# Windowed attention with sinks and an MLP on one core: scores and values of batches 2 to 4 in one run of 64x64 quarters

## The chip, the core and the metric

The kernel runs on one core of a Trainium2 chip. The metric is the device time of one execution in microseconds. TensorE (PE) multiplies matrices; VectorE (DVE), ScalarE (ACT) and GpSimd (POOL) work on elements; SyncE (SP) and POOL issue most of the DMA transfers. Below, a *quarter* is a matmul whose weights are 64 rows by 64 columns; TensorE's array of 128 by 128 holds four of them side by side (two row halves, two column halves).

## The reference

```python
batch, n_heads, seq, head_dim = (4, 8, 768, 64)
n_sink, window = (4, 128)
...
scores = scale * np.matmul(q, k.transpose(0, 1, 3, 2))
keep = is_sink | in_window        # key < 4, or 0 <= query - key < 128
scores = np.where(keep, scores, -1000000000.0)
a = softmax(scores)
attn = np.matmul(a, v)            # heads side by side: x is [4, 768, 512]
...
xn = (x - mu) / np.sqrt(var + 1e-06) * g_ln
ch = np.maximum(xn @ w_ch1, 0.0) @ w_ch2     # 512 -> 2048 -> 512
return (x + ch).astype(np.float32)
```

Each query sees its own and at most the 127 keys before it, and the four sink keys at the start of the sequence.

## The kernel before

A *tile* is 128 positions of one batch with all 8 heads (24 tiles, six to a batch); a *chunk* c is two tiles (12 chunks, three to a batch, R = c % 3). Batch 1 is chunks 0 to 2, batches 2 to 4 are chunks 3 to 11. Everything is bf16 on TensorE, with sums in fp32.

Nothing runs in the order of the code. Each step is handed to a planner (`Plan.op`) with its engine, a modelled duration, a priority, and what it reads and writes. `Plan.run` then goes through a simulated time, gives each step its buffer out of a ring, and so fixes one order for every engine before the program is built. A smaller priority goes first. `at(c, step)` is 16 c - 8 plus a constant of `PAR`, so one chunk is 16 units, about one matmul group of 0.87 us each. A step of the engine PE with a priority of `strict` or more must be the next of all TensorE steps.

For each chunk: `chunk` loads q, k and v (POOL, with the cast to bf16; `nat` has 8 buffers, `vn` 7). From chunk 4 on (`by_dma`) SP turns q and k into `kT` and `qT` by DMA transposes (four for a chunk, L542), after the second scores of the chunk before. `attend` (L728) makes the scores transposed, keys on partitions: in a batch's first chunk with weights of 64 by 128 (L750), in the others with quarters in bands (`bands`, L663: 24 matmuls of 64, 128 or 192 columns for each half of the heads). L754 makes the scores of the sink keys. ScalarE takes exp (L764), VectorE masks (L768). `value` multiplies the probabilities by V: for each head two matmuls with full 128x128 weights and 65 columns (L798; the 65th column of V is one, which gives the sum), and two of 260 columns for the sinks (L793, `vs`). VectorE divides (L811, L813), takes mean and variance (L817, L819) and subtracts the mean (L821); from chunk 3 on SP transposes the outcome into `xnt`.

`mlp` multiplies by the first weight (L867: 64 matmuls of 256 columns for a chunk, relu by L877) and by the second (L896: 32 of 512 columns), adds x (L904) and stores (L908). The attention of chunk c is laid between the matmuls of the MLP of chunks c - 2 and c - 1. PSUM has eight banks: two `pair` buffers of two banks for scores and values, four `one` buffers for all else.

## Time and profile before

| | us |
|---|---|
| median of 3 runs | 220.79 (220.29 to 220.82) |
| the profiled execution | 220.3 |
| its span, first to last instruction | 218.7 |
| granted TensorE clock, mean | 0.997 |
| PE busy | 211.0 (97%) |
| DVE, ACT, POOL busy | 117.9, 108.2, 90.2 |
| the chain that ended last: L896, L867 | 39%, 35% of the span |
| the same: L798, L663, L793, L750 | 4%, 3%, 1%, 1% |

Matmuls are pipelined: a matmul's recorded length reaches beyond the start of the next, so the pace of TensorE is read from the starts. The chain is followed back from the last instruction, at each step to what released it or to the instruction before on its engine. The strip shows 40 equal slices of the span (5.5 us each), in tenths.

### The profile page before, as it was taken

What the parts mean: (1) busy time and instruction counts of PE and PEld (TensorE: products, weight loads), DVE (VectorE), ACT (ScalarE), POOL (GpSimd) and SP (SyncE); (2) the same over time, 40 slices, a digit from 0 to 9 for tenths busy, and PEclk for the clock granted to TensorE, in tenths of its full rate; (3) what the DMA queues carried; (4) which work ended last, traced back from release to release, by engine and by line L of the source; (5) the groups of instructions that cost most, each with busy time, mean ns of one, the idle gap of its engine ahead of it and who ended that gap; (6) DMA issues with size and microseconds to landing.
All of it is one profiled execution on the core that took longest, in us unless ns stands there. A gap on an engine that the chain in (4) does not pass through costs nothing.

```text
span 218.7 us, 5474 instructions
## 1 busy us (share of the span) xinstructions
PE 211.0 (97%) x2233; PEld 144.6 (66%) x2233; DVE 117.9 (54%) x269; ACT 108.2 (49%) x162; POOL 90.2 (41%) x131
## 2 busy tenths in 40 slices
PE   6889999999999999999999999999999999999993
PEld 2557875764965964964965964964965965965852
DVE  5489845595797725725715815725716715732011
ACT  3768465145447447445546447445546447441610
POOL 7998673798091813463550722570110110120000
PEclk9999999999999999999999999999999999999998
DMA  5999999999999999799897999997523421121103
GB/s 155 163 183 207 176 206 197 156 211 154 179 159 163 139 120 129 100 160 145 139 135 116 133 115 129 135 140 106 129 40 98 107 41 48 51 48 51 48 12 101
DMA packets 108576, 27.47 MB, mean 126 GB/s; under 512 B 99200, under 2 KB 105600, under 8 KB 108544
## 3 DMA queue, kind: packets, MB, share of 16 engines
q0 software_dynamic: 74944, 13.11, 83.7%
q1 hardware_dynamic: 32544, 13.41, 30.2%
q10 hardware_dynamic: 1056, 0.52, 0.9%
q8 instruction: 19, 0.31, 0.6%
q14 instruction: 13, 0.11, 0.2%
HBM read 27.30 MB, written 6.29 MB: 154 GB/s over the span
## 4 chain that ended last, share of the span: by engine, by line
PE 90%; DVE 6%; issue 1%; ACT 1%; DVEq 0%
PE one L896 39%; PE one L867 35%; PE pair L798 4%; PE pair L663 3%; PE pair L962 2%; PE pair L793 1%; DVE st L817 1%; PE pair L750 1%; DVE x L813 1%; DVE xc L821 1%; DVE xnt L845 1%; PE one L639 1%; PE one L860 1%; PE one L834 1%; PE one L754 1%
## 5 line engine op out<-in xcount | busy, mean ns | idle before, releaser
L896 PE MATMUL one<-w,h 128*128 128x512 bf16 (+1 forms) x400 | 89.0, 371 | 0.0
L877 ACT ACTIVATE h<-one 128x512 bf16<-128x512 f32 x95 | 56.6, 598 | 59.1 <-PE one L867 50.7
L867 PE MATMUL one<-xnt,w 128*128 128x256 bf16 x704 | 82.4, 273 | 0.0
L867 PEld LDWEIGHTS <-w 128*128 128x128 bf16 x704 | 67.4, 98 | 10.2
L896 PEld LDWEIGHTS <-h 128*128 128x128 bf16 x400 | 37.3, 98 | 38.2 <-issue 0.9
L768 DVE TENSOR_TENSOR pe<-pe,mask 128x1024 bf16<-128x1024 bf16 (+1 forms) x40 | 26.0, 649 | 54.7 <-ACT pe L764 53.8
L764 ACT ACTIVATE pe<-pair 128x1024 bf16<-128x1024 f32 (+1 forms) x40 | 36.2, 957 | 33.4 <-PE pair L663 21.6
L625 POOL DMA_DIRECT2D nat<-in_k_dram x16 | 14.2, 890 | 36.8 <-DMA kT<-nat 28.1
L904 DVE SCALAR_TENSOR_TENSOR ot<-one,st,x 128x512 f32<-128x512 f32 (+1 forms) x25 | 18.1, 725 | 15.2 <-PE one L896 15.1
L826 POOL TENSOR_SCALAR st<-st 128x1 f32<-128x1 f32 x24 | 7.1, 297 | 43.4 <-DVE st L819 42.2
L548 POOL DMA_DIRECT2D vn<-in_v_dram x24 | 21.9, 921 | 3.3 <-DMA w<-in_moe_w_ch_dram 3.1
L625 POOL DMA_DIRECT2D nat<-in_q_dram x16 | 14.6, 913 | 12.9 <-DMA qT<-nat 12.0
L817 DVE BATCH_NORM_STATS2 st<-x 128x6 f32<-128x512 bf16 x24 | 16.7, 695 | 0.8
L798 PEld LDWEIGHTS <-pe 128*128 128x128 bf16 x352 | 14.0, 97 | 2.1 <-ACT pe L709 0.6
L827 POOL TENSOR_TENSOR st<-st,mhalf 128x1 f32<-128x1 f32 x24 | 14.3, 596 | 2.0
L813 DVE TENSOR_TENSOR x<-pair,rec 128x512 bf16<-128x512 f32 x20 | 13.8, 691 | 0.7
L798 PE MATMUL pair<-vn,pe 128*128 128x65 bf16 x296 | 12.2, 193 | 0.0
L663 PEld LDWEIGHTS <-kT 64*64 64x64 bf16 x400 | 6.2, 107 | 6.3 <-issue 6.1
L821 DVE TENSOR_SCALAR xc<-x,st 128x512 bf16<-128x512 bf16 x24 | 9.3, 389 | 0.9
L811 DVE RECIPROCAL rec<-pair 128x8 f32<-128x8 f32 x20 | 4.0, 202 | 9.7 <-PE pair L798 9.7
L709 ACT ACTIVATE pe<-pair 128x1024 bf16<-128x1024 f32 (+1 forms) x8 | 7.3, 919 | 3.5 <-PE pair L663 2.1
L663 PE MATMUL pair<-qT,kT 64*64 64x64 bf16 (+2 forms) x400 | 8.9, 219 | 0.1
(87 smaller groups left out, 127.4 us busy)
## 6 DMA issues: line engine op xcount, KB each, us to landing
out_dram<-ot SPq DMA_DIRECT2D x23, 256.0 KB
w<-in_moe_w_ch_dram POOLq DMA_DIRECT2D x8, 512.0 KB, 12.9
vn<-in_v_dram POOLq DMA_DIRECT2D x24, 128.0 KB, 6.3
nat<-in_k_dram POOLq DMA_DIRECT2D x22, 128.0 KB, 6.1
nat<-in_q_dram POOLq DMA_DIRECT2D x22, 128.0 KB, 6.2
natf<-in_k_dram SPq DMA_DIRECT2D x2, 256.0 KB
natf<-in_q_dram ACTq DMA_DIRECT2D x2, 256.0 KB
xnt<-xc SPq DMA_TRANSPOSE x18
```

Source lines behind the costliest of these rows:

```text
L548: P.op(f"vld{t}", {"POOL": (0.87, 0.9)}, prio, lambda e: G.dma_start(bv.t[:, :, 0:64], v[b, :, 128 * r:128 * (r + 1), :].rearrange("h p d ...
L625: lambda e, nat=nat, ap=ap: G.dma_start(nat.t, ap), writes=[nat], dma=SW)
L663: nc.tensor.matmul(pp.t[64 * kh:64 * kh + 64, h2, col + off:col + off + n], lhsT=kt.t[rs, hp, k0 + 64 * kh:k0 + 64 * kh + 64], rhs=qT.t[rs ...
L764: P.op(f"ex{c}{hp}", {"ACT": act(2 * n)}, d + 0.1 + 0.05 * j, lambda e, pp=pp, pb=pb: nc.scalar.activation(pb.t[:, :, 0:n], pp.t[:, :, 0:n ...
L768: V.tensor_tensor(pb.t[:, :, 0:n], pb.t[:, :, 0:n], mm, op=ALU.min if R else ALU.mult),
L798: nc.tensor.matmul(bank(h // 4)[:, 65 * (h % 4):65 * (h % 4) + 65], lhsT=part(h, n), rhs=vn_b[tv].t[:, h, :], start=(not R and h % 4 == 0 ...
L813: P.op(f"x{t}{run[0]}", {"DVE": dve(512 * share)}, dd + 0.11, lambda e, pv=pv, rc=rc, run=run: V.tensor_tensor(x.t[:, 256 * run[0]:256 * r ...
L817: P.op(f"bn{t}", {"DVE": fix(0.60)}, d + 0.12, lambda e: V.bn_stats(st.t[:, 8:14], x.t), reads=[x], writes=[st, mv])
L867: nc.tensor.matmul(ph.t[:, 256 * s:256 * s + 256], lhsT=w1[ht // 4][:, j, 128 * (ht % 4):128 * (ht % 4 + 1)], rhs=xnt.t[:, j, :], start=j ...
L877: nc.scalar.activation(hb.t, ph.t, AF.Relu)
L896: nc.tensor.matmul(pc.t[:, 0:wd], lhsT=(h1[2 * s + i].t[:, 128 * ii:128 * ii + 128] if by_tile else h1[ht // 2].t[:, 256 * (ht % 2) + 128 ...
L904: V.scalar_tensor_tensor(ot.t[:, sl], in0=pc.t[:, 0:wd], scalar=st.t[:, 16:17], in1=x.t[:, sl], op0=ALU.mult, op1=ALU.add),
```

## The change

For tiles 6 to 23 (batches 2 to 4) `attend` and `value` give way to `block(t)`: one run of TensorE with the sink values and values of tile t - 1 and then the scores of tile t, all as 64x64 quarters; on the even tile the scores of the chunk's sink keys follow. `block(NT)` holds the last tile's values alone. A tile's scores are 48 quarters of 64 columns (24 for a batch's first tile), its values 48 of 65 columns (24 for the first) and four of 260 for the sinks. The 64x64 parts that the window masks wholly are not computed any more. For this a quarter needs V in the other half of the partitions too: SP copies each V tile with its halves exchanged (`vsw`, two DMAs for each of 18 tiles), and the same for the sinks' `vs` (`vs_s`, six DMAs).

PSUM gets a third pair out of the banks of `one` 0 and 1, which other steps may borrow (`lent`) unless a block is due; the second MLP product of chunks 2 and up uses `one` 2 and 3 alone (`acc`). Masks are multiplied (`band`, `first`) over two thirds of a tile's probabilities. `block` has priority 16 c - 16 for the even and 16 c - 10 for the odd tile; the scores had 16 c - 13 and 16 c - 10, the values 16 c - 6 and 16 c - 5.

Also changed: loads of chunks after 4 start no earlier than 58 us in the plan; chunk 4's transposes don't wait for chunk 3's scores; the gain vector is loaded as 4 rows and transposed on TensorE; the planner's constants `strict`, `SHARED` and `HW_T`. Cut to its core, the diff is:

```diff
-    SHARED = 36.0
+    SHARED = 62.0
...
+HW_V = (0.2, 0.8, 1.2)
...
-HW_T = (0.10, 0.8, 0.8)
+HW_T = (0.02, 0.8, 0.8)
...
-PAR = dict(strict=40.0, win=0.4, tr=-8.0, sc=-5.0, sc1=-2.0, av=2.0, trx=9.0, by_dma=4, x_by_dma=3,
-           w1p=(1.6, 2.6, 2.7, 2.8), pm=3, w2p=(4.5, 4.51, 4.52, 4.53), apart=2, vs0=(2.0, 13.0), by_tile=1, vp=(0.0, 0.1, 2.0, 2.1, 4.55, 4.56), ld1=0.05)
+PAR = dict(strict=400.0, late=58.0, win=0.4, tr=-8.0, sc=-5.0, sc1=-2.0, av=2.0, blk=-8.0, step=6.0, trx=9.0, by_dma=4, x_by_dma=3,
+           w1p=(1.6, 2.6, 2.7, 2.8), pm=3, w2p=(4.5, 4.51, 4.52, 4.53), apart=2, vs0=(2.0, 13.0), by_tile=1, vp=(0.0, 0.1, 2.0, 2.1, 4.55, 4.56), ld1=0.05, gtt=1.25)
 
...
-    pairs = [psum.tile([128, 2, 512], FP32, name=f"pair{i}") for i in range(2)]
-    ones = [psum.tile([128, 512], FP32, name=f"one{i}") for i in range(4)]
-    P.ring("pair", [Slot(pairs[i], f"pair{i}", banks[2 * i:2 * i + 2]) for i in range(2)])
-    P.ring("one", [Slot(ones[i], f"one{i}", [banks[4 + i]]) for i in range(4)])
+    pairs = [psum.tile([128, 2, 512], FP32, name=f"pair{i}") for i in range(3)]
+    ones = [pairs[2][:, i, :] for i in range(2)] + [psum.tile([128, 512], FP32, name=f"one{i}") for i in range(2, 4)]
+    P.ring("two", [Slot(pairs[i], f"two{i}", banks[2 * i:2 * i + 2]) for i in range(2)])
+    P.ring("pair", [Slot(pairs[i], f"pair{i}", banks[2 * i:2 * i + 2]) for i in range(3)])
+    P.ring("one", [Slot(ones[i], f"one{i}", [banks[4 + i]], rank=0, lent=i < 2) for i in range(4)])
+    P.ring("acc", [Slot(ones[i], f"acc{i}", [banks[4 + i]]) for i in range(2, 4)])
...
+    ring("vsw", 6, [128, H, 65], BF16)
...
-    P.op("gt", {"SP": (0.4, 0.4)}, 3.0, lambda e: nc.sync.dma_start(gt, moe_g_ln.rearrange("(j p) -> p j", p=128)),
-         writes=[Bc["gt"]], dma=HW_T)
+    gr_b, gt_p = Buf("g_rows"), Buf("gtp", "one")
+    P.op("gt", {"SP": (0.4, 0.4)}, 3.0, lambda e: nc.sync.dma_start(g_rows, moe_g_ln.rearrange("(j p) -> j p", p=128)),
+         writes=[gr_b], dma=HW_T)
+    P.op("gtt", pe(0.1), PAR["gtt"], lambda e: nc.tensor.transpose(gt_p.t[:, 0:NDM], g_rows, ident_f[0:NDM, 0:NDM]),
+         reads=[gr_b, Bc["ident_f"]], writes=[gt_p])
+    P.op("gtc", {"DVE": fix(0.07)}, PAR["gtt"] + 0.1, lambda e: V.tensor_copy(gt, gt_p.t[:, 0:NDM]), reads=[gt_p], writes=[Bc["gt"]])
...
+    Bvt = [None] + [Buf(f"vt{b}") for b in range(1, B)]
+    for b in range(1, B):
+        for g in range(2):
+            P.op(f"vt{b}{g}", {"SP": (0.35, 0.4)}, 48.0 * b - 19.5, lambda e, b=b, g=g: nc.sync.dma_start(
+                vs_s[b][64 * g:64 * g + 64], vs[b][64 * (1 - g):64 * (1 - g) + 64]), reads=[Bvs[b]], writes=[Bvt[b]], dma=HW_V)
...
-            writes=[bv], dma=SW, after=list(ones_of.values()))
+            writes=[bv], dma=SW, after=list(ones_of.values()), nb=PAR["late"] if t > 2 * PAR["by_dma"] + 1 else 0.0)
+
+    vS_b = {}
+
+    def swap_v(t, prio):
+        src, dst, parts = vn_b[t], Buf(f"vS{t}", "vsw"), []
+        vS_b[t] = dst
+        for g in range(2):
+            P.op(f"vsw{t}{g}", {"SP": (0.35, 0.4)}, prio + 0.01 * g, lambda e, g=g: nc.sync.dma_start(
+                dst.t[64 * g:64 * g + 64], src.t[64 * (1 - g):64 * (1 - g) + 64]), reads=[src], writes=[dst], dma=HW_V)
 
...
-                             lambda e, nat=nat, ap=ap: G.dma_start(nat.t, ap), writes=[nat], dma=SW)
+                             lambda e, nat=nat, ap=ap: G.dma_start(nat.t, ap), writes=[nat], dma=SW, nb=PAR["late"] if c > PAR["by_dma"] else 0.0)
...
-                             after=[scores[c - 1]])
+                             after=[scores[c - 1]] if c > PAR["by_dma"] else [])
...
+            if c >= RC:
+                swap_v(2 * c + i, ld + 8.0 + 0.1 * i)
...
+    held = {}
+
+    def block(t):
+        c, i, b, r = t // 2, t % 2, t // RB, t % RB
+        d = at(c, "blk") + PAR["step"] * i
+        last = held.get(t - 1)
+        reads, writes, hold = [], [], []
+        if t < NT:
+            kT, qT, kprev = kT_b[c], qT_b[c], (kT_b[c] if i else kT_b[c - 1])
+            own, old = slice(128 * i, 128 * i + 128), slice(128 * (1 - i), 128 * (1 - i) + 128)
+            n_pair = 2
+            pps, pes = [Buf(f"s{t}{j}", "pair") for j in range(n_pair)], [Buf(f"p{t}{j}", "pe") for j in range(n_pair)]
+            sinks = i == 0
+            if sinks:
+                held["ps", c] = Buf(f"ps{c}", "ps")
+            ps = held["ps", c] if r else None
+            pp_s = Buf(f"pss{c}", "one") if sinks else None
+            made = [Buf(f"st{t}", "st"), Buf(f"x{t}", "x"), Buf(f"xc{t}", "xc")]
+            held[t] = dict(ps=ps, made=made, pes=pes)
+            reads += [kT, qT] + ([kprev] if r and not i else []) + ([kts_b[b]] if sinks else [])
+            writes += pps + ([pp_s] if sinks else [])
+            hold += pes + ([held["ps", c]] if sinks else [])
+        if last:
+            lc, li, lb, lr = (t - 1) // 2, (t - 1) % 2, (t - 1) // RB, (t - 1) % RB
+            po = Buf(f"po{t - 1}", "pair")
+            reads += last["pes"] + ([last["ps"], Bvs[lb], Bvt[lb]] if last["ps"] else [])
+            reads += [z[u] for u in ([t - 2, t - 1] if lr else [t - 1]) for z in (vn_b, vS_b)]
+            writes += [po]
+            hold += last["made"]
+
+        def quarters(r):
+            return [[(h, qh, qh ^ (h // 4), s) for h in range(4 * u, 4 * u + 4) for s in ((0, 1, 2) if r else (1, 2) if qh else (2,))]
+                    for u in range(2) for qh in range(2)]
+
+        def turns(lists):
+            return [l[n] for n in range(max(map(len, lists))) for l in lists if n < len(l)]
+
+        def keys(qh, s):
+            return (s == 2 or (s == 1 and qh == 1)), (qh if s != 1 else 1 - qh)
+
+        def go(e):
+            if last and last["ps"]:
+                for u in range(2):
+                    for qh in range(2):
+                        g = qh ^ u
+                        rs = slice(64 * g, 64 * g + 64)
+                        nc.tensor.matmul(po.t[64 * qh:64 * qh + 64, u, 0:260],
+                                         lhsT=last["ps"].t[rs, 128 * u + 64 * li:128 * u + 64 * li + 64],
+                                         rhs=(vs if g == u else vs_s)[lb][rs].rearrange("p h c -> p (h c)"),
+                                         start=True, stop=False, skip_group_check=True)
+            begun = set()
+            for h, qh, g, s in turns(quarters(lr)) if last else ():
+                is_own, kh = keys(qh, s)
+                u, rs = t - 1 if is_own else t - 2, slice(64 * g, 64 * g + 64)
+                at_h = 192 * (2 * (h % 2) + h // 2 % 2) + 64 * s
+                nc.tensor.matmul(po.t[64 * qh:64 * qh + 64, h // 4, 65 * (h % 4):65 * (h % 4) + 65],
+                                 lhsT=last["pes"][h // 4].t.rearrange("p a b -> p (a b)")[rs, at_h:at_h + 64],
+                                 rhs=(vn_b if kh == g else vS_b)[u].t[rs, h, :],
+                                 start=not last["ps"] and (h // 4, qh) not in begun, stop=s == 2, skip_group_check=True)
+                begun.add((h // 4, qh))
+            if t == NT:
+                return
+            for hp in range(HP):
+                for s in (0, 1, 2) if r else (1, 2):
+                    for qh in (0, 1) if r or s == 2 else (1,):
+                        is_own, kh = keys(qh, s)
+                        kt, k0 = (kT, own.start) if is_own else (kprev, old.start)
+                        j, col = qh ^ (hp // 2), 192 * (hp % 2) + 64 * s
+                        for h2 in range(2):
+                            rs = slice(64 * h2, 64 * h2 + 64)
+                            nc.tensor.matmul(pps[hp // 2].t[64 * j:64 * j + 64, h2, col:col + 64],
+                                             lhsT=kt.t[rs, hp, k0 + 64 * kh:k0 + 64 * kh + 64],
+                                             rhs=qT.t[rs, hp, own.start + 64 * qh:own.start + 64 * qh + 64],
+                                             start=hp % 2 == 0 and s == (0 if r else 2 - qh), stop=True, skip_group_check=True)
+            if sinks:
+                for hp in range(HP):
+                    for qh in range(2):
+                        u = hp // 2
+                        p0 = 64 * (qh ^ u) + 32 * (hp % 2)
+                        nc.tensor.matmul(pp_s.t[p0:p0 + 32, 128 * u:128 * u + 128], lhsT=kts_b[b].t[:, hp, :],
+                                         rhs=qT.t[:, hp, :].rearrange("p (i u c) -> p u i c", i=2, u=2)[:, qh],
+                                         start=True, stop=True, skip_group_check=True)
+        cost = (0.0 if t == NT else 0.33 if r else 0.22) + (0.0 if not last else (0.34 if lr else 0.23) + (0.115 if last["ps"] else 0.0))
+        end = t < NT and sinks
+        P.op(f"sc{t}", pe(cost + (0.21 if end else 0)), d, go, reads=reads, writes=writes, hold=hold, mode=("q", "c") if end else "q")
+        if t < NT:
+            scores[c] = P.ops[-1]
+            for j in range(n_pair):
...
+                P.op(f"ex{t}_{j}", {"ACT": act(full)}, d + 0.1 + 0.05 * j, ex, reads=[pps[j]], writes=[pes[j]])
+                P.op(f"mk{t}_{j}", {"DVE": dve(512 if r else 256, 0.52)}, d + 0.2 + 0.05 * j, mk, reads=[Bc["band"]], rw=[pes[j]])
...
+            P.op(f"rc{t - 1}", {"DVE": fix(0.115)}, d + 0.05, lambda e: V.reciprocal(rc(), pv()[:, :, :, 64]),
+                 reads=[po], writes=[rcb, one_rc])
+            P.op(f"x{t - 1}", {"DVE": dve(512)}, d + 0.06, lambda e: V.tensor_tensor(
+                x.t.rearrange("p (a h c) -> p a h c", a=2, c=64), pv()[:, :, :, 0:64],
+                rc().unsqueeze(3).to_broadcast([128, 2, 4, 64]), op=ALU.mult), reads=[po, one_rc], writes=[x])
+            normalise(lc, li, d - 0.06, st, x, xc)
...
-                pc = Buf(f"pc{t}{f}", "one")
+                pc = Buf(f"pc{t}{f}", "one" if c < 2 else "acc")
...
+        elif c < RC:
+            attend(c)
         else:
-            attend(c)
+            block(2 * c)
+            block(2 * c + 1)
+    block(NT)
```

115 lines of the change are left out of this document (73 added, 42 removed).

## The prediction

> **What bounds the kernel now.** I read the page first: where the span goes, the strip of 40 slices, the chain.
>
> ```profile
> span 218.7 us, 5474 instructions
> PE 211.0 (97%) x2233; PEld 144.6 (66%) x2233; DVE 117.9 (54%) x269; ACT 108.2 (49%) x162; POOL 90.2 (41%) x131
> PE   6889999999999999999999999999999999999993
> PEclk9999999999999999999999999999999999999998
> DMA  5999999999999999799897999997523421121103
> PE 90%; DVE 6%; issue 1%; ACT 1%; DVEq 0%
> ```
>
> TensorE is busy in every slice from the fourth on, at the full granted clock, and is 90% of the chain. A busy TensorE can hide waits, so next the list of TensorE's waits:
>
> ```profile
> PE pair L962 <- DVE one_e L458: 1.8, 1, 1.8
> PE one L834 <- DVE xc L821: 0.9, 2, 0.6
> PE pair L684 <- ACT pe L709: 0.4, 1, 0.4
> PE pair L703 <- ACT qT L554: 0.2, 1, 0.2
> ```
>
> All four lie before 26 us. From there to 215 us TensorE waits for nobody, so only TensorE's own work can shorten this stretch, and no other engine's can. The timeline gives that work. A later chunk of a batch (columns: start, length of the group, engine, line, names, count):
>
> ```profile
> 113.22 0.81 PE L896 MATMUL one<-w,h 128*128 128x512 bf16 x3
> 113.96 0.53 PE L663 MATMUL pair<-qT,kT 64*64 64x64 bf16 x24
> 114.43 0.29 PE L754 MATMUL one<-qT,kts 128*32 128x256 bf16 x4
> 114.65 2.76 PE L896 MATMUL one<-w,h 128*128 128x512 bf16 x12
> 117.34 0.53 PE L663 MATMUL pair<-qT,kT 64*64 64x64 bf16 x24
> 117.81 1.90 PE L896 MATMUL one<-w,h 128*128 128x512 bf16 x8
> 119.55 1.91 PE L867 MATMUL one<-xnt,w 128*128 128x256 bf16 x16
> 121.29 0.39 PE L793 MATMUL pair<-vs,ps 128*128 128x260 bf16 x2
> 121.52 0.65 PE L798 MATMUL pair<-vn,pe 128*128 128x65 bf16 x16
> 122.00 0.27 PE L867 MATMUL one<-xnt,w 128*128 128x256 bf16 x1
> ```
>
> Successive L896 start 216 ns apart, L867 109 ns. Three L896 from 113.22 end at 113.87; the next starts at 114.65. So scores with sinks cost 0.78 us, the second half (114.65 + 12 x 0.216 to 117.81) 0.56, and one tile's values (121.30 to 122.00) 0.707. A later chunk's attention takes 0.781 + 0.557 + 2 x 0.707 = 2.752 us of TensorE. A batch's first chunk, read in the same way at 98 to 107 us, takes 0.533 + 0.532 (L750) + 0.259 + 0.485 (L798) = 1.809. Batches 2 to 4: 6 x 2.752 + 3 x 1.809 = 21.94 us.
>
> **Prices.** In the run of 117.34 the matmuls start within 343 ns of each other; 93 ns pass between the last L896's slot and the first of them, and 94 after the last one's slot. So entering and leaving the quarter mode costs 187 ns together, and the sinks (two mode changes and 256 columns) add 0.781 - 0.557 = 224. Single starts of 64-column quarters in the same quarter are 27 to 28 ns apart (114.134 and 114.162; 114.159 and 114.187), with the next weights loaded underneath (load at 114.160, its matmul at 114.187). The two row halves start 3 ns apart and the column halves overlap, so four quarters run at once. 65-column L798 start 29.2 ns apart, L793's 260 columns take 110.
>
> **The new runs, by columns.** Scores of a tile: 48 quarters of 64 columns, 12 to each quarter of the array, 12 x 28 = 336 ns; a batch's first tile 24, of which one quarter gets 8: 224. Values: 48 of 65 columns, 12 x 29.2 = 350; first tile 8 x 29.2 = 234. Sink values: four of 260 columns side by side, 110. Frame: 187 plus 28 for the first weights = 215. Sink scores: eight of 128 columns, four at once, 224 + 4.
> - Later chunk: 215 + 336 + 350 + 110 + 228 = 1239 and 215 + 336 + 350 + 110 = 1011; 2.250 against 2.752. Six of these: -3.01 us.
> - First chunk of batches 3 and 4: 215 + 224 + 350 + 110 + 228 = 1127 and 215 + 336 + 234 = 785; 1.912 against 1.809. Two: +0.21.
> - First chunk of batch 2 (no values queued): 667 + 785 = 1.452. One: -0.36.
> - The closing run for the last tile's values: 215 + 350 + 110, +0.68.
>
> Sum -2.5 us. It comes from the values alone: a tile needs 12 slots of 65 columns instead of 16, and 260 sink columns instead of 520. The score columns (384 per pair of heads) stay, and so do the five mode changes of a later chunk.
>
> **What lies beside other work.** Exponentials go from four of 1021 ns to four of about 808 (the 768-column row) per later chunk, masks get shorter: ScalarE and VectorE are 49% and 54% busy, so nothing is gained. Larger constants (L485 to L488 took 0.53, 0.47, 0.21, 0.48; the new ones are twelve such, 2.5 to 5 us) run from 28 us, where VectorE is busy 11.2 of the 18 us from 30 to 48; without that cover up to 1 us, through the evictions L554 at 28.3 and 29.6. The gain vector arrives in 4 rows instead of 512 elements, with one transpose and one small copy: nothing after 26 us, and before it the chain runs through VectorE; I take 0, bounds -0.3 to +0.3. The 42 swap copies go on SP's queue, past the transposes of kT, qT and xnt and the stores. A store took 0.33 to 0.53 us there, so 4 x 0.4 per chunk beside six transposes of 1.2 in 16.6 us: room enough. A swap that waits for a late V (6.3 us to landing, at most 12.7) holds up the transposes behind it; I take 0, and up to 2 us between 40 and 65 us, where DMA is full. The delayed loads (58 us) and the planner's other constants move order only, and TensorE has no idle to win by that.
>
> PSUM is tighter: an even block holds three pairs and one bank, seven of eight. It falls into L896 work, which holds one bank for 16 x 0.216 = 3.5 us; the block's evictions (rc 0.20, x 0.69; two exponentials 0.81 each) fit into that. I take 0; uncovered, one relu (0.60) per chunk, 9 x 0.6 = 5.4, at most.
>
> **Rivals.**
> 1. *Issue instead of columns.* The old runs have 24 quarters, the new ones 100. PE's sequencer runs ahead of the array by a bounded queue: its separate waits at 54.08, 103.14, 143.98 and 152.20 us came 17 matmuls ahead of the one executing. The first 17 of a run therefore cost nothing, the other 83 are fed at the sequencer's rate. The old trace bounds that rate only from above: after the sequencer stood at 9.399, weights and matmuls followed so that the seventh instruction started 48 ns after the first (8 ns each), and at 15.32 to 15.45 at least 14 instructions passed in 132 ns (9 ns each). So a load and a matmul cost between 3 ns (the starts inside a queue) and 16 to 18; columns need 7 to 8. At 16 a full run takes 83 x 16 = 1.33 us for 0.80: 12 x 0.53 + 2 x 0.26 + 3 x 0.31 + 0.1 = +7.9, net +5.4, 226.2 us. It decides from 11.8 ns on. For it: no run of before is long enough to show this rate. Against: at 9.506 the spacing is the same to 1 ns as at 7.800, where the queue was full. Between the ends the cost falls evenly, from nothing to 226.2. Chance 0.11.
>
> The Trainium skill (TensorEngine Tiling (Array Packing), Instruction Overhead) gives each matmul about 60 cycles and advises against tiling a dimension that is already small. By that figure, at 2.4 GHz, a run of 100 would be an estimated 2.5 us, and the change would be a heavy loss; the 24 starts in 343 ns (14 ns each) already disagree with it.
>
> 2. *Two row halves in one PSUM bank.* Values put quarters of both row halves into one bank at once, in different partitions; old quarters had a bank for each row half. If that serializes, each full run's 460 ns doubles: 15 x 0.46 + 3 x 0.23 = +7.6, net +5.1, 225.9 us. Against: L754's four column strips write one bank and start 3 ns apart. Chance 0.04. The Trainium skill says in the same page (Gotcha 1: PSUM Pressure) that different row tiles can't access one bank at the same time; no run here shows it.
>
> 3. *TensorE waits for qT.* From the odd block of a chunk to the next even block lie 8 L896 and 64 L867: 1.73 + 6.99 = 8.7 us. In the old order the way from the second scores to the next first ones was 68.82 to 81.58, 12.8 us. In it SP sends four transposes (the trace of SP's queue: start, length):
>
> ```profile
> 68.43 1.23 SPq L542 DMA_TRANSPOSE kT<-nat  x1
> 69.76 1.21 SPq L542 DMA_TRANSPOSE qT<-nat  x1
> 71.07 1.21 SPq L542 DMA_TRANSPOSE kT<-nat  x1
> ...
> 73.00 1.26 SPq L542 DMA_TRANSPOSE qT<-nat  x1
> ```
>
> The last landed (the trace's DMA semaphores) at 80.6, right behind a load that POOL had issued at 72.72 into a buffer the first transposes had freed. After the second scores' end the last transposes of the seven later DMA-fed chunks landed by 11.8, 10.4, 9.1, 11.2, 8.6, 7.1 and 6.4 us. If that recurs against 8.7, TensorE waits 3.1 + 1.7 + 0.4 + 2.5 = 7.7: net +5.2, 226.0 us. It decides once these waits sum to 2.5 us. Against: with no load just ahead a transpose lands in 2.4 us (13 of 32 did, in 2.4 to 2.5), which makes 7.0 with the 4.6 us to the last issue, and fits; and the loads' times are moved by the change (58 us, no wait for the first chunk's transposes). For: the loads are released by the transposes themselves. The odd tile's xnt has a like path: 2.7 us to xc, then 2.4 to 6 to land, against 32 L896 and an odd block, 7.9. Chance 0.23. Into the forecast I take the smallest of the four, rounded to 0.5 us; the weak half of this rival is the same-or-little-gain case, 219.8 to 221.4, chance 0.09.
>
> **The numbers.** The profiled execution took 220.3 (span 218.7 and 1.6 around it); -2.5 and +0.5 of waits for qT make 218.3. The median of the runs stands 0.5 higher, 220.8, so 218.8. The forecast's own range: 27 ns for each quarter, no ramp and no wait give 1.2 less, small costs and waits 1.0 more: 217.2 to 219.8, chance 0.50; 0.03 lies below. Rivals 1, 2 and 3 have 0.11, 0.04 and 0.23, the little-gain case 0.09. The range runs from 216.9 to 224.4: it takes in the cheaper halves of rivals 1 and 3 and leaves out the dearer ones and rival 2. Under 0.3% (0.7 us, what a measurement can tell) counts as the same: faster 0.50 + 0.03 + 0.03 of the little-gain case, same its other 0.06 and 0.01 of rival 1, slower the rest, 0.37.
>
> **What would show it.** Right: 48 score quarters in about 0.34 us and a run of 100 in 0.80 to 0.85; the whole block 1.0 to 1.25; no PE wait after 26 us. Issue: the first 17 matmuls dense, later starts an even 10 to 18 ns apart whatever their columns. Bank: values at twice the spacing of scores. Waits: L867 idle on xnt, or a block on an eviction. I am wrong if TensorE's time between two chunks of a batch (16.67 us now) does not fall to about 16.17.

## The result and the profile after

The changed kernel takes 242.0 us (median of 4 runs, 238.9 to 245.3) against 220.5 in the same comparison: ratio 1.093 [1.082, 1.104]. The forecast was 218.8, the range up to 224.4, and the dearest rival 226.2. So the direction, the range and every rival's size were wrong. A profile shows one execution: that of the changed kernel is the fastest of its four, and what the other three lose beyond it is in no profile; those of e1, e11 and e12 are of executions slower than their medians.

From the page of its profiled execution (238.9 us, span 237.4), the lines that answer to those shown of before:

```profile
span 237.4 us, 7670 instructions
PE 213.7 (90%) x3302; PEld 147.5 (62%) x3302; DVE 108.9 (46%) x277; ACT 101.0 (43%) x167; POOL 91.6 (39%) x131
PE   6898899999999779989949999989959999999990
PEclk9999999999999999999999999999979999999999
DMA  6999999999999999999999999999531612303011
PE 68%; DMA 12%; SPq 7%; DVE 7%; ACT 3%; issue 1%; DVEq 0%
```

TensorE's strip, without a gap in before from the fourth slice on, has holes now (7, 7, 4, 5), and the chain runs through DMA and SyncE's queue for 19% of the span. The waits of TensorE name the holes (us in total, times, longest):

```profile
PE one L959 <- DMA qT<-nat: 10.2, 5, 3.1
PE pair L926 <- ACT h L1032: 2.1, 7, 0.3
PE pair L1121 <- DVE one_e L466: 1.8, 1, 1.8
PE pair L820 <- ACT h L1032: 1.0, 1, 1.0
PE pair L673 <- ACT h L1032: 0.7, 1, 0.7
```

L959 are the sink scores, the only matmuls of an even block that read the qT of the whole chunk. One such place in TensorE's timeline, the start of a block and its end:

```profile
80.83 0.27 PE L926 MATMUL pair<-vs,ps 64*64 64x260 bf16 x1 [0.30 <-ACT h L1032]
...
81.34 0.66 PE L950 MATMUL pair<-qT,kT 64*64 64x64 bf16 x48
84.86 0.30 PE L959 MATMUL one<-qT,kts 128*32 128x128 bf16 x8 [2.86 <-DMA qT<-nat]
85.09 1.25 PE L1051 MATMUL one<-w,h 128*128 128x512 bf16 x5
```

And the queue of SyncE that sent this qT, after the odd block that began at 70.48 and ended at 71.74:

```profile
71.14 0.54 SPq L1063 DMA_DIRECT2D out_dram<-ot  x1
71.74 1.77 SPq L583 DMA_DIRECT2D vsw<-vn  x3
73.60 2.01 SPq L567 DMA_TRANSPOSE kT<-nat  x1
75.78 1.19 SPq L567 DMA_TRANSPOSE qT<-nat  x1
77.06 1.22 SPq L567 DMA_TRANSPOSE xnt<-xc  x1
78.37 1.22 SPq L567 DMA_TRANSPOSE kT<-nat  x1
79.68 0.54 SPq L1063 DMA_DIRECT2D out_dram<-ot  x1
80.32 1.23 SPq L567 DMA_TRANSPOSE qT<-nat  x1
```

Three copies of V (L583, `vsw`) go first, then a transpose of xnt and a store come in between; the last qT leaves at 80.32 and lands at 84.82. From 71.74 to 81.55 the queue never pauses for more than 0.17 us: it has 9.8 us of issues for a way of 8.7. Two more of the five waits (3.25 and 2.56 us) follow a place where the queue stood still with a copy whose V had not landed; ahead of the transposes of the two short ones (1.18 and 1.04) no copy went. SyncE's waits list that standing:

```profile
SPq L583 <- DMA vn<-in_v_dram: 8.5, 2, 4.9
```

The two traces by stretch (us; "front" is the start of the second chunk's second product, "runs" is the time that attention takes out of the products' slots after it, "between" is lost inside the products):

| | before | after | difference |
|---|---|---|---|
| front | 46.05 | 47.91 | +1.86 |
| runs: waits for qT (3.05 + 1.18 + 3.25 + 1.04 + 2.56) | 0 | 11.08 | +11.08 |
| runs: all else | 22.59 | 24.87 | +2.28 |
| between (six L1051 at half clock, 176.67 to 178.4) | 0.27 | 1.57 | +1.30 |
| last matmul to the end of the span | 4.05 | 6.23 | +2.18 |
| span | 218.68 | 237.38 | +18.70 |

The forecast had "runs" at 20.1. More than half of the loss is the wait of the third rival; the rest was in no rival. Of the +2.28, 2.1 are the seven waits of L926 for a relu.

### The profile page after: what moved, and what is told of

Read it like the earlier page. It is cut to its first block, busy times and chain, and to the rows that moved or that the text cites. A ratio compares the mean times of both kernels' runs of the same rounds, so it can differ in the third digit from the quotient of the medians.

```text
span 237.4 us, 7670 instructions
## 1 busy us (share of the span) xinstructions
PE 213.7 (90%) x3302; PEld 147.5 (62%) x3302; DVE 108.9 (46%) x277; ACT 101.0 (43%) x167; POOL 91.6 (39%) x131
## 4 chain that ended last, share of the span: by engine, by line
PE 68%; DMA 12%; SPq 7%; DVE 7%; ACT 3%; issue 1%; DVEq 0%
PE one L1051 33%; PE one L1022 10%; PE pair L1022 10%; DMA qT<-nat 10%; SPq L567 6%; PE pair L935 2%; ACT h L1032 2%; PE pair L950 2%; DMA natf<-in_k_dram 2%; PE pair L1015 2%; DVE st L848 1%; PE pair L1051 1%; PE pair L926 1%; SPq L1063 1%; PE one L959 1%
## 5 line engine op out<-in xcount | busy, mean ns | idle before, releaser
L1051 PE MATMUL one<-w,h 128*128 128x512 bf16 (+1 forms) x384 | 85.3, 375 | 0.0
L1051 PEld LDWEIGHTS <-h 128*128 128x128 bf16 x400 | 37.6, 98 | 40.3 <-issue 2.0
L1022 PE MATMUL one<-xnt,w 128*128 128x256 bf16 x360 | 44.5, 273 | 0.0
L974 ACT ACTIVATE pe<-pair 128x768 bf16<-128x768 f32 x30 | 22.7, 808 | 47.8 <-PE pair L950 47.8
L1022 PE MATMUL pair<-xnt,w 128*128 128x256 bf16 x344 | 41.3, 273 | 0.0
L1032 ACT ACTIVATE h<-pair 128x512 bf16<-128x512 f32 x47 | 25.8, 595 | 36.3 <-PE pair L1022 34.0
L1032 ACT ACTIVATE h<-one 128x512 bf16<-128x512 f32 x48 | 28.7, 601 | 20.7 <-PE one L1022 18.6
L573 POOL DMA_DIRECT2D vn<-in_v_dram x24 | 21.8, 916 | 13.1 <-PE pair L950 10.0
L959 PE MATMUL one<-qT,kts 128*32 128x128 bf16 x64 | 2.5, 232 | 10.2 <-DMA qT<-nat 10.2
L982 DVE TENSOR_TENSOR pe<-pe,band 128x512 bf16<-128x512 bf16 x30 | 11.3, 418 | 0.0
L950 PE MATMUL pair<-qT,kT 64*64 64x64 bf16 x792 | 11.2, 197 | 0.0
L935 PEld LDWEIGHTS <-pe 64*64 64x64 bf16 x792 | 9.4, 107 | 1.1 <-issue 1.1
L950 PEld LDWEIGHTS <-kT 64*64 64x64 bf16 x792 | 9.5, 105 | 0.5 <-issue 0.4
```

The lines of the kernel that those rows point to most:

```text
L573: P.op(f"vld{t}", {"POOL": (0.87, 0.9)}, prio, lambda e: G.dma_start(bv.t[:, :, 0:64], v[b, :, 128 * r:128 * (r + 1), :].rearrange("h p d ...
L935: nc.tensor.matmul(po.t[64 * qh:64 * qh + 64, h // 4, 65 * (h % 4):65 * (h % 4) + 65], lhsT=last["pes"][h // 4].t.rearrange("p a b -> p (a ...
L950: nc.tensor.matmul(pps[hp // 2].t[64 * j:64 * j + 64, h2, col:col + 64], lhsT=kt.t[rs, hp, k0 + 64 * kh:k0 + 64 * kh + 64], rhs=qT.t[rs, h ...
L974: nc.scalar.activation(dst.rearrange("p (a b) -> p a b", a=2), src, AF.Exp, scale=scale)
L1022: nc.tensor.matmul(ph.t[:, 256 * s:256 * s + 256], lhsT=w1[ht // 4][:, j, 128 * (ht % 4):128 * (ht % 4 + 1)], rhs=xnt.t[:, j, :], start=j ...
L1032: nc.scalar.activation(hb.t, ph.t, AF.Relu)
```

## The experiments

First reasons: (A) the transposes of a chunk are late because SP sends copies, xnt and stores in the 8.7 us that the new order leaves; (B) the shorter way alone does it; (C) the quarters cost more than columns. A fourth, which settled the rest, came up only after e13. Below, a letter in brackets is one of these reasons; a letter without is the theory of that name in the expectation printed above it.

### The way of qT: e1 to e4

**e1_early**: the changed kernel, no transpose waits for the scores of the chunk before.

```
-   after=[scores[c - 1]] if c > PAR["by_dma"] else [])
+   after=[])
```

> The changed kernel, in which no transposes of q and k wait for the scores of the chunk before any more (only free buffers hold them). Theory A (TensorE waits for the last qT, 11.1 us in five waits, with some 1.3 us at half clock behind them): these waits go, 238.9 - 12.4 = 226 to 227 us. Rival B (the 64x64 runs themselves are slow, by issue or by a shared bank): the blocks stay as long as they are without the waits, 1.2 to 1.4 us, and what is lost is in them; then less than 3 us of difference, 236 or more. Rival C (the queue of SP as a whole is too full): the transposes come early but xnt or the swapped V come late instead; a new wait at L1022 or L935 and over 230 us.

241.0 us, ratio 1.091 [1.084, 1.098]. The waits for qT are gone, and TensorE stands as long for xnt, behind the same queue:

```profile
PE one L1022 <- DMA xnt<-xc: 10.0, 2, 6.2
```

**e2_before_sc8**: the kernel before with the old first scores 3 us earlier.

```
-   sc=-5.0
+   sc=-8.0
```

> The kernel before, with the first scores of each chunk three units earlier (priority 16 c - 16 for 16 c - 13), where the changed kernel has them; all else as before. Theory A: the way from the second scores to the next first ones falls from 12.8 to 10.2 us, against last landings of 11.8, 10.4, 9.1, 11.2, 8.6, 7.1 and 6.4 us: TensorE waits 1.6 + 0.2 + 1.0 = 2.8 us, 223 to 224 us. Rival B (quarters alone): no difference, 220.5.

222.0, ratio 1.007 [1.005, 1.009]: three gaps before the scores of 0.37, 0.89 and 0.52 us, less than A had. A way shortened from 12.8 to 10.2 us costs some 1.6 us in the old kernel, not 21. The new one has 8.7, which this run does not reach; e3 has it without copies. (B) is real and small.

**e3_noswap**: the changed kernel without the 42 copies; products read V and the sink values as they are, so half of them multiply the wrong keys (the lines for the sinks are left out here).

```
-   swap_v(2 * c + i, ld + 8.0 + 0.1 * i)
-   rhs=(vn_b if kh == g else vS_b)[u].t[rs, h, :]
+   rhs=vn_b[u].t[rs, h, :]
```

> The changed kernel without the 42 swap copies; the quarters that read the swapped V or sinks read the straight ones, so the values are sums over other keys. Theory A with the swaps as its cause (42 x 0.5 us on SP ahead of the transposes, and their packets): the waits for qT fall to under 4 us, 230 or less. Theory A with the order as its cause (the way is 8.7 us, and the last transposes go behind loads): the waits stay at 7 to 11 us, 235 to 239.

230.7, ratio 1.047 [1.040, 1.053]: 11.3 us of the 21.5 go with the copies; waits for qT fall to 1.13 + 0.88 + 0.70. That is what (B) costs at a way of 8.7 us: 2.7 us, about as much as the two waits of the changed kernel that had no copy ahead of them.

```profile
PE one L954 <- DMA qT<-nat: 2.2, 3, 0.9
```

**e4_early_blk5**: e1 with each block due 3 us later.

```
-   blk=-8.0
+   blk=-5.0
```

> As the first of these, with the block three units later (priority 16 c - 13 and 16 c - 7), after three groups of L896. Theory A: qT has 2.6 us more, and the two borrowed banks are free when the block begins, so L926 no longer waits 0.3 us for a relu in each chunk (2.4 us in all): 223 to 225. Against: xnt of the odd tile has 2.6 us less (5.3 us from the end of the values to L1022, where xc and the transposes need 5.1 to 8.7); then L1022 waits up to 3 us in each chunk and it is over 230.

254.1, ratio 1.155 [1.149, 1.162]: later values make xc later, and the waits for xnt grow to 13.1 + 5.2 us. Room for qT is taken from xnt.

### Where the copies cost: e5, e6, e9

**e5_before_swaps**: the kernel before with the 36 copies of V alone (not the six of the sink values, which the expectation counts in), read by nobody.

```
+   for g in range(2):
+       P.op(f"vsw{t}{g}", {"SP": (0.35, 0.4)}, prio + 0.01 * g, lambda e, g=g: nc.sync.dma_start(
+           dst.t[64 * g:64 * g + 64], src.t[64 * (1 - g):64 * (1 - g) + 64]), reads=[src], writes=[dst], dma=HW_V)
```

> The kernel before, plus the 42 swap copies of V on SyncE's queue, into buffers that nothing reads; blocks, order of TensorE and gates as before. Theory A, the copies hold up the transposes behind them on SP's queue wherever they stand: the last qT transpose of the seven later chunks had 1.0 to 2.9 us to spare in most chunks of before, and the copies of one chunk take 2 to 3 us of the queue, so TensorE waits for qT or xnt by 0.5 to 1 us in several chunks: 222 to 226 us. Theory B, the copies hurt only because the new order leaves 8.7 us instead of 12.8 for the way: no TensorE wait after 26 us and a time within 0.7 us of before.

235.6, ratio 1.070 [1.062, 1.077]: A, and far beyond its range: 15.5 us where it had 2 to 6. All other engines, and the rest of SP's queue, keep the order of before. What a copy of 0.57 us (median) does to the queue is seen in SP's waits, and then in its timeline (the copies are L557 here, the transposes L544):

```profile
SPq L557 <- DMA vn<-in_v_dram: 46.1, 13, 8.1
```

```profile
98.61 1.23 SPq L544 DMA_TRANSPOSE xnt<-xc  x1
104.26 1.11 SPq L557 DMA_DIRECT2D vsw<-vn  x2
105.46 1.31 SPq L544 DMA_TRANSPOSE xnt<-xc  x1
```

From 99.84 to 104.26 the queue stands with a copy whose V has not landed, and the second xnt of the chunk stands behind it. TensorE's timeline pays:

```profile
110.48 0.72 PE L877 MATMUL one<-xnt,w 128*128 128x256 bf16 x5 [3.40 <-DMA xnt<-xc]
```

In the changed kernel such standing is 8.5 us, not 46.1: there the copies also cost by their own time, 1.9 us of the short way at 71.74.

**e6_swap_act**: the changed kernel, copies issued by ScalarE.

```
-   {"SP": (0.35, 0.4)}, ... nc.sync.dma_start(
+   {"ACT": (0.35, 0.4)}, ... nc.scalar.dma_start(
```

> The changed kernel with the 42 swap copies issued from ScalarE's queue in place of SyncE's; same bytes, same buffers. Theory A, what made qT late was the order on SyncE's queue: TensorE's waits for qT fall from 11.1 us to about 3 as in the run without copies, 230 to 233 us. Theory B, it is the transfers themselves, which fill the DMA engines whoever issues them: waits for qT of 8 to 11 us stay, 237 to 242 us. Theory C, a copy that waits for its V now holds up ScalarE's relus and exponentials: TensorE waits for h or pe by over 3 us, and the time is above 235 us with qT waits below 4.

232.3, ratio 1.055 [1.049, 1.060]: A. With the same bytes moved, waits for qT fall to 1.6 us (as the list of waits counts them, 10.2 in the changed kernel). Part of C shows: two waits of the first product, 1.7 and 1.1 us, for a relu and an exponential held up on ScalarE.

**e9_even_swlate**: the changed kernel, transposes released by the even block and copies behind them.

```
-   scores[c] = P.ops[-1]
+   if not i:
+       scores[c] = P.ops[-1]
...
-   swap_v(2 * c + i, ld + 8.0 + 0.1 * i)
+   swap_v(2 * c + i, ld + 15.0 + 0.1 * i)
```

> The changed kernel with two edits to the order of SyncE's queue: the transposes of a chunk are released by the even block of the chunk before in place of its odd block, which gives them some 16 us instead of 8.7, and a chunk's copies come after its four transposes. Theory A, the way from the odd block to the next even one was too short for four transposes with copies among them: the 11.1 us of waits for qT go and little comes for them, 229 to 233 us. Theory B, transposes and loads that start earlier push the loads of the next chunk against the transposes of xnt, as in the run without a gate: TensorE waits 4 us or more for xnt, 235 to 241 us.

229.0, ratio 1.041 [1.035, 1.048]: A. No wait for qT, one of 1.15 us for xnt (0.98 in the list of waits). The two edits to the order of one queue are worth 13 us together; no run parts them.

```profile
PE one L1023 <- DMA xnt<-xc: 1.0, 1, 1.0
```

### Columns or issue: e7

**e7_cols33**: values in full runs take 33 columns for 65 (half of the dimensions are left out there).

```
-   rhs=(vn_b if kh == g else vS_b)[u].t[rs, h, :],
+   rhs=(vn_b if kh == g else vS_b)[u].t[rs, h, 32 if last["ps"] else 0:65],
```

> The changed kernel with 33 of the 65 columns in each quarter of a tile's values where the sinks are present (32 of the 64 dimensions are left out); the same number of matmuls and weight loads. Columns: 12 slots of 29 ns become 12 of about 15, so the run of 100 shortens from 923 ns between its first and last start to about 745, and the closing run likewise by 0.18 us. Issue: the starts cannot come closer than the 8.3 to 8.5 ns of a load and a matmul that the second half of the run showed, so a run of 100 keeps at least 830 to 880 ns.

First the changed kernel's run at 182.74, first values and first scores, then the same of e7:

```profile
182.88 0.19 PE L935 MATMUL pair<-vn,pe 64*64 64x65 bf16 x2
...
183.25 0.60 PE L950 MATMUL pair<-qT,kT 64*64 64x64 bf16 x48
```

```profile
182.99 0.18 PE L935 MATMUL pair<-vn,pe 64*64 64x33 bf16 x2
...
183.36 0.60 PE L950 MATMUL pair<-qT,kT 64*64 64x64 bf16 x48
```

0.37 us in both: 48 quarters take 364 ns from first to last start with 65 columns and 362 with 33. The run lasts 922 ns for 923. So it isn't columns. The starts come in fours at first; from the 32nd to 40th quarter of a run on many are 8 to 9 ns apart, with single steps up to 118 ns, and the 48 scores behind the values take 410 to 592 ns in the changed kernel. (Whole run: 239.3 us, one execution.) The Trainium skill (TensorEngine Tiling (Array Packing), Instruction Overhead) says that a matmul of one column lasts as long as one of 60; inside a quarter this agrees (32 ns on average from one start to the next in the same quarter, at 33 and at 65 columns), but four quarters run side by side, so a matmul costs 7.7 ns of TensorE.

### What was left, first guesses: e10 to e13, e15

All on e9. **e10_bands**, **e11_blk7**, **e12_pad** change one line each, **e13_all** all three; **e15_late0** lets the held loads go.

```
-   writes=[Bc["band"]], nb=28.0)
+   writes=[Bc["band"]], nb=40.0)          # e10
-   blk=-8.0
+   blk=-7.0                               # e11
-   nc.tensor.matmul(o, lhsT=junk[:, 0:128], rhs=junk, ...)
+   for z in range(8):                     # e12
+       nc.tensor.matmul(o[:, 64 * z:64 * z + 64], lhsT=junk[:, 0:128], rhs=junk[:, 64 * z:64 * z + 64], ...)
-   late=58.0
+   late=0.0                               # e15
```

> The reordered version (run e9: 229.0 us) with one more edit: the twelve instructions that make the mask bands may start at 40 us in place of 28. In e9 they hold VectorE from 27.6 to 32.1, the copies of kT and qT and the relus queue on ScalarE meanwhile, and the second product of the second chunk starts at 48.59 us where before had 46.05. Theory A, the bands make that delay: the start comes back to 46.5 to 47.2 us and the time to 227 to 227.8. Theory B, the front is late for another reason (order of the first chunks, banks lent to the front): the start stays within 0.5 us of 48.6 and the time within 0.7 of 229.0.

233.7, ratio 1.054 [1.046, 1.061]. The start is 48.68, where e9 has 47.94 (the expectation's 48.59 is late by three matmuls that the trace lacks), and the wait of 0.7 at L673 stays although VectorE is free then: the bands aren't it. Dearer, with a wait of 3.1 for xnt.

> The reordered version (run e9: 229.0 us) with one more edit: each block of scores and values is due 1 us later, which puts four second products between the first products and the even block. In e9 the even blocks wait 0.3 us each, seven times, for the relu that empties the banks lent to the first product. Theory A, these waits vanish and nothing takes their place: 226.5 to 227.5 us. Theory B, TensorE waits instead later in the chunk, for xnt or for a relu, because the values come later: 228.5 us or more, with new waits of 1.5 us or more.

232.3, ratio 1.044 [1.039, 1.049]: B. The 0.3 us for a relu turn up in front of the first product instead (eight times), and 3.8 us for xnt.

> The reordered version (run e9: 229.0 us) with one more edit: each of the nine warm-up matmuls of 512 columns on zeros in the first 5 us is cut into eight of 64, which adds 63 matmuls with their loads, some 8 KB, half a block, to TensorE's instructions ahead of the rest. In e9, and in the changed kernel, TensorE stands still twice after its last matmul while a 16 KB block of its own instructions arrives (2.6 and 2.9 us; once, 2.6, in before). Theory A, that the last step crosses from one block into the next is an accident of length: the way from the last matmul to the end falls from 6.15 to about 4 us and the time to 226.7 to 227.2. Theory B, the longer program has this wait wherever the border lies: the end stays at 5.5 us or more and the time at 228.5 to 229.5.

231.5, ratio 1.043 [1.035, 1.050]. The end falls to 4.16 us as A says, and the total doesn't follow: a wait of 3.1 us for xnt, and two of TensorE for nothing that the profile shows, in the midst of runs:

```profile
94.82 0.64 PE L950 MATMUL pair<-qT,kT 64*64 64x64 bf16 x46
96.64 0.22 PE L950 MATMUL pair<-qT,kT 64*64 64x64 bf16 x2 [1.18 <-issue]
```

In the trace a 16 KB block of TensorE's own instructions moves from 93.43 to 95.10, and the array goes on 1.5 us behind it. The other stand, of 0.8 us, ends at 88.80, also 1.5 us behind such a block.

> The reordered version (run e9: 229.0 us) with the three edits together: bands from 40 us, blocks due 1 us later, longer warm-up. If what is left over before were only the front (2.5 us), the relu waits (2.1), the end (2.1) and one wait for xnt (1.1), this would come to about 222 us, and the runs of quarters would then still cost TensorE more than the runs they replaced. If the runs of quarters were cheaper than the old ones, as predicted by columns, it would be below 220. If the edits disturb each other, 224 to 228.

234.7, ratio 1.067 [1.063, 1.070]: above all three readings. The end is 4.09; the front is 48.67.

> The reordered version (run e9: 229.0 us) with one more edit: the loads of chunks 5 and later may start when their buffers come free, not only from 58 us on. Theory A, the loads that were held back pile up behind 58 us and pass ahead of the transposes of xnt at 71 to 95 us: the waits for xnt (1.1 us in e9, 3.1 to 3.9 in e10 to e12) go, 226 to 228 us. Theory B, earlier loads only meet the weights' loads and the copies sooner: waits for xnt, qT or V of 2 us or more remain and the time is 228.5 us or more.

232.5, ratio 1.056 [1.054, 1.058]: B. A wait of 3.1 us for xnt begins at 73.4 us; with the loads held back there is one there too, of 1.15 in e9 and 3.1 in e12.

### Two banks in one tile: e14, e16 to e18

The front of the changed kernel held the clue. ScalarE's and TensorE's timelines:

```profile
27.82 0.60 ACT L1032 ACTIVATE h<-one 128x512 bf16<-128x512 f32 x1
29.04 0.60 ACT L1032 ACTIVATE h<-pair 128x512 bf16<-128x512 f32 x1 [0.63 <-PE pair L673]
```

```profile
27.72 1.05 PE L1015 MATMUL pair<-xnt,w 128*128 128x128 bf16 x16
28.61 0.39 PE L673 MATMUL pair<-ident,nat 128*128 128x128 bf16 x4
29.68 0.38 PE L673 MATMUL pair<-ident,nat 128*128 128x128 bf16 x4 [0.69 <-ACT h L1032]
```

The relu of what L1015 wrote waits for transposes into another bank, and the next transposes wait for that relu. The two banks are the halves of one tile: `ones = [pairs[2][:, i, :] for i in range(2)] + ...`.

**e14_alias**: the kernel before, with this alone.

```
-   ones = [psum.tile([128, 512], FP32, name=f"one{i}") for i in range(4)]
+   both = psum.tile([128, 2, 512], FP32, name="both"); ones = [both[:, i, :] for i in range(2)] + [psum.tile([128, 512], FP32, name=f"one{i}") for i in range(2, 4)]
```

> The kernel before with one edit: two of its four single PSUM banks are the halves of one tile of two banks, as in the changed kernel; the same eight banks, and the same order of instructions on every engine is planned. In the changed kernel a relu of one half (29.07 us) waited for transposes into the other half, and the next transposes (29.68) for that relu. Theory A, instructions on the two halves wait for each other as if they shared data: waits of TensorE for relus appear from 15 us on, the second chunk's second product starts at 47.5 to 49 us in place of 46.05, and the time is 222 to 228 us, since the later chunks use the same banks. Theory B, the halves are kept apart and the front is late for its order: no new wait, and a time within 0.7 us of before.

229.0, ratio 1.040 [1.038, 1.042]: A, a little above its range. The same banks, the same planned order, and the waits bear the tile's name:

```profile
PE both L896 <- ACT h L877: 1.4, 2, 0.7
PE both L896 <- DVE ot L904: 0.9, 2, 0.5
PE both L860 <- ACT h L877: 0.8, 1, 0.8
PE both L867 <- DVE kT L554: 0.6, 1, 0.6
```

The front is at 49.34 for 46.05. Each wait ends with a named releaser's semaphore, which speaks for an order in the program and not for a conflict inside PSUM.

**e17_split_only** (on the changed kernel) and **e16_split** (on e9) make the third pair of two tiles; a block that gets it does its exponential, reciprocal and product bank by bank. **e18_split_blk7** is e16 with `blk=-7.0`.

```
-   pairs = [psum.tile([128, 2, 512], FP32, name=f"pair{i}") for i in range(3)]
-   ones = [pairs[2][:, i, :] for i in range(2)] + [psum.tile([128, 512], FP32, name=f"one{i}") for i in range(2, 4)]
+   pairs = [psum.tile([128, 2, 512], FP32, name=f"pair{i}") for i in range(2)]
+   ones = [psum.tile([128, 512], FP32, name=f"one{i}") for i in range(4)]
+   pairs.append(Halves(ones[0], ones[1]))
```

> The changed kernel with the third pair of banks made of two tiles again, and the order of SyncE's queue as the change has it. Theory A, costs of the shared tile and of late transposes add up: 242.0 - 8 = 232 to 236 us, with TensorE's waits for qT of 9 to 14 us. Theory B, a TensorE that is quicker by the tile only waits the longer for qT: 237 us or more.

236.9, ratio 1.068 [1.059, 1.077], at the border of A and B: the waits for qT are 11.7 us (six) for 11.1.

> The reordered version (run e9: 229.0 us) with the third pair of banks made of two tiles again; where a block uses that pair, its exponential, reciprocal and product are done bank by bank. Theory A, the shared tile makes nearly all that is left (the kernel before lost 9.0 us by it alone): 219.5 to 222.5 us, the second chunk's second product starting at 46 to 47 us. Theory B, the runs of quarters cost several us by themselves: 223.5 to 227 us.

227.1, ratio 1.029 [1.027, 1.031], just above B's range, and for another reason than B's. The front is at 45.70, and the waits for relus before the even blocks, which I had taken for real, are gone. What is left by its trace: three waits for xnt (1.67 + 1.28 + 1.11; the profile puts the last down to VectorE, but it ends at 107.90, and the xnt landed at 107.86), and an end of 6.97 us. The runs take 23.08 us, 0.5 more than in before.

> The version of run e16 with each block due 1 us later, so that four second products stand between the first products and the even block. Theory A, the waits of 0.3 us for a relu before the even blocks go, and nothing takes their place: 1.5 to 2.5 us below e16. Theory B, the later values make xnt late, as they did in e11: as e16 or slower, with waits for xnt of 1.5 us or more.

224.3, ratio 1.019 [1.017, 1.021]: 2.8 better than e16, more than A had, though e16 had no relu wait left to lose, and with B's waits for xnt (0.88 and 2.60). Of the 3.0 us between the two spans, 2.5 is the end (4.43 for 6.97) and 0.6 the waits for xnt. Its span is 4.17 above before: front -0.36, runs +0.54, between +3.62 (3.48 the two waits), end +0.38. This is the best version of the change, and slower than before.

### Without the copies: e19

**e19_split_noswap**: e18 with the edit of e3.

> The version of run e18 without the copies of V with exchanged halves and of the sink values; the products that need them read V and the sink values as they stand, so half of them multiply the wrong keys, at the same cost. Theory A, the two waits for xnt (0.9 and 2.6 us in e18) come from the copies, and the runs cost TensorE 0.5 us more than the old ones: no wait over 1 us after 50 us, and 220.3 to 221.5 us, level with the kernel before. Theory B, the waits come from the order of transposes and loads: 1.5 us or more of waits for xnt or qT stay, 222.5 to 224.5 us. Theory C, the gain by columns is there once the rest is gone: 217.5 to 219.5 us.

223.5, ratio 1.012 [1.007, 1.016]; the profiled execution 222.5, which is B: runs 22.71 us (before 22.59), front +0.41, end +0.10, and one wait of 1.45 us before a first product, from 71.87 to 73.31. The profile puts it down to VectorE:

```profile
PE one L1040 <- DVE pe L995: 1.3, 1, 1.3
```

But the xnt of that product left at 66.98 and landed at 73.27, 0.04 us before the start, as in the waits for xnt of e16 and e18. So it is a wait for xnt once more, without any copy on the queue; of ten loads that POOL had issued from 57.3 to 65.2 us the last landed at 72.5. Nothing of the gain by columns is there (C). The executions lie between 221.4 and 224.7; what moves them isn't known.

## Why the prediction was wrong, point by point

- **"The 42 swap copies ... room enough"**, taken at 0 with up to 2 us. This step failed worst. I added up queue time over a whole chunk (4 x 0.4 us in 16.6), though the transposes had only the 8.7 us of rival 3: from 71.74 us on, copies, transposes, xnt and a store need 9.8 there. And I never followed what stands behind a copy that waits. Taking the copies out gives 11.3 us back (e3); putting 36 of them into the kernel before costs 15.5 (235.6 - 220.1). The step even named a swap behind a late V, with 2 us at most: SP stood so for 46.1 us in e5 and for 8.5 in the changed kernel.
- **"PSUM is tighter ... I take 0"**, at most 5.4. I priced buffers, while the cost lay in how they are made: the halves of one tile wait for each other, 8.9 us in the kernel before (e14), 5.1 in the changed kernel (e17), with a front 1.4 us earlier. The line stood in the diff. The front's +1.9, for which I had allowed the bands "up to 1 us" and the gain vector 0.3, is this for the most part: 46.47 in e17 and 45.70 in e16, with bands and gain vector as changed; e10 had cleared the bands.
- **Rival 3**, chance 0.23, was right in its place and its path: five waits at the even blocks, 11.1 us for 7.7. Its cause was half right. A shorter way by itself costs 1.6 (e2) to 2.7 (e3); with the copies in it, it costs 11. The reading beside it, that an odd tile's xnt lands in 2.4 to 6 us, was a little low: one took 6.5 in before (61.52 to 68.00).
- **"Sum -2.5 us"**, by columns: wrong by 2.6 to 3.0. With all else out of the way the runs take 22.7 to 23.1 us, not 20.1. A run's sinks and values are near their price (0.51 us from 182.74 to 183.25; 28 + 110 + 350 ns priced), but e7 shows that the price is of the matmul and not of its columns. The 48 scores behind them take 408 to 603 ns from first to last start in e18 where 336 were priced. So the runs of a later chunk take 1.39 to 1.47 and 1.14 to 1.34 us there, for 1.239 and 1.011 priced: together 2.67 on average, for 2.250 priced and 2.752 in before. Fewer columns in more, smaller matmuls bought nothing.
- **Rival 1** had the picture ("the first 17 matmuls dense, later starts an even 10 to 18 ns apart") below its lower end: 8 to 9 ns for many, with single steps above, 8.7 to 12.8 on average over the 48 scores (e18), and from the 32nd to 40th start on, not the 17th. Its price of 226.2 was for 16 ns. It is the place in the run and not the kind of quarter: 24 scores that begin a run (49.96 in the changed kernel) still come in fours, in 189 ns.
- **Rival 2** is refuted: values of both row halves in one bank keep 31 to 33 ns a slot (e7, and the changed kernel), nowhere near twice the 29.2 priced. The Trainium skill (TensorEngine Tiling (Array Packing), Gotcha 1: PSUM Pressure) has it that different row tiles can't access one bank at once; here, with the row halves in different partitions of the bank, no run shows a cost.
- **The end**, +2.2, was in no term. TensorE's own instructions come in 16 KB blocks by queue 8 (19 of them in before with 2233 matmuls, 27 here with 3302: lines `q8 instruction: 19, 0.31` and `q8 instruction: 27, 0.44` of the pages). After its last matmul TensorE stands from 231.15 to 233.95 for a block, as before did from 214.63 to 217.26, and once more from 234.81 to 237.15. Half a block more of instructions ahead takes the second wait away (4.16 in e12), so it is an accident of length. The Trainium skill (Runtime: NRT & Kernel Launch, Instruction fetch mechanics) says that a taken branch out of the blocks at hand waits for a fetch; both kernels branch over a fallback at this place, and the first of the waits agrees: in the traces TensorE's branch ends at 217.20 in before and at 233.90 here, each 1.5 us behind a block.
- **"I am wrong if TensorE's time between two chunks of a batch (16.67 us now) does not fall to about 16.17"**: it did not. From even block to even block it was 20.03 and 20.66 us in batches 3 and 4; the 16.10 of batch 2 is luck, since its wait comes behind the second of them. In e18, in the two batches without a wait, 16.67 and 16.45 for 16.67 in before.

What stays open: what makes xnt late between 70 and 108 us in the repaired versions (0.9 to 3.3 us, from one order to the next; the loads are likely, but holding them back or not did not settle it, and e19 shows that the copies are not needed for it), and what spaces the second half of a run, the sequencer or the loading of weights.

## What to carry to other kernels

When a transfer is added to a queue, take the shortest stretch in which something on that queue must be done and add up all that is issued in it. Then price the wait of a transfer that stands still, with everything queued behind it. The queue's load over a longer stretch shows neither. When a diff makes two buffers views of one tile, count every instruction on the one half as ordered with those on the other until a trace shows otherwise. Before cutting matmuls into quarters, count instructions: at 7.7 to 12.8 ns on average for each weight load with its matmul, going from 65 columns to 33 gained nothing here.

## What the runs showed of the hardware that I had not expected

- A quarter of 64 rows with 33 columns takes as long as one with 65: 362 and 364 ns for 48 of them.
- TensorE's instructions seem to run out inside a run of quarters: 1.38 us between two starts at 95.26 us in e12 and 1.14 at 73.86 in e10, each just after a 16 KB block of them had moved. The array goes on 1.5 and 1.3 us behind the block's last packet, as at the end of the kernel; no run tests it otherwise. The Trainium skill (Runtime: NRT & Kernel Launch, Instruction fetch mechanics) calls the crossing from one block to the next mostly hidden; at most blocks of these traces it is, and here it was not.
- After TensorE had waited for 2.4 us (173.5 to 175.9) in the changed kernel, its clock went to half for a while: the six L1051 after it start 430 ns apart in place of 216. Two longer waits of the same run (2.9 and 3.1 us) were followed by nothing of the kind. The view by windows (PE busy first, then the granted clock behind the busy times):

```profile
176.60:178.40 1.80, 1.80 (x6) 0.62 (x5) 0.00 (x0) 0.24 (x1) 0.00 (x0) 0.50 0.38 77
```
